# Later load landings, float32r products for the layer norm's sums, and split V loads in an attention, MLP and mixer kernel

## The chip, the cores and the metric

One core of a Trainium2 chip runs the whole computation as one program. The metric is the device time of one execution, in microseconds, as the median of several runs; a profiled execution gives the trace. TensorE (PE) does the matrix products, its weight loads (PEld) go beside them, VectorE (DVE), ScalarE (ACT) and GpSimd (POOL) do the element-wise work, and SyncE (SP) issues nearly all DMAs from one queue in order.

## The reference

Batch 4, 8 heads, 576 positions, head size 64, model width 512, hidden width 2048.

```python
scores = q @ k^T / sqrt(64);  bias = -(cum[i] - cum[j]) with cum = cumsum(max(s, 0))
attn = softmax(causal(scores + min(bias, 0)));  x = attn @ v          # heads side by side: x is (4, 576, 512)
xn = (x - mean(x)) / sqrt(var(x) + 1e-6) * g
x = x + relu(xn @ w1a) @ w2a                                           # first MLP, called layer 0
u = x + ((x^T @ U) @ V)^T                                              # mixer over the 576 positions, rank 32
out = u + relu(u @ w1b) @ w2b                                          # second MLP, called layer 1
```

## The kernel before

Work is cut into blocks of positions: for each batch b a block Ab of 256 positions and a block Bb of 320; in layer 1, blocks C0 to C3 of 512 positions and one block T0 that collects the last 64 positions of all four batches. Precision comes from splitting a float32 value into a float32r part (hi, a rounded copy) and the rest (lo, a subtraction); a product is then three float32r products, hi·hi, lo·hi and hi·lo. The helper `split` (line 384) issues the copy (`copy`, ACT line 381 or DVE line 382) and the subtraction (`tt`, DVE line 386 or POOL line 388).

The MLPs run as steps. One step is one block times one tile of 128 hidden units: `mlp1` (lines 1396 to 1398) forms the hidden tile in PSUM, ACT and DVE (lines 1402 and 1403) make its hi and lo parts, and `mlp2` (lines 1416 to 1418, or 1453 to 1455) adds its share of the output two steps later. Layer 0 has 128 steps in the order A0, A1 (steps 0 to 31, in turns of 8), A2, A3 (32 to 63), B0 (64 to 79), B1, B2, B3 (to 127). Layer 1 follows with C0, C1, C2, T0, C3. The attention and the layer norm of a later block run between the steps of earlier ones: the table `AT` gives the steps between which a block's attention is spread, and `LN` the step at which its layer norm is put. A0 and A1 have their attention ahead of the first step.

No engine's order is written by hand. `Plan` collects all operations with their data dependences, an assumed duration, a priority and the engines that may do each one. `plan` simulates them and keeps, for each engine, an order and a choice of engine; `latest` walks back from the end and gives each operation the latest start that delays nothing, and `issue` plans again (`PASSES` = 4 times) with those as priorities, less a head start `HEAD` in microseconds, found by the priority with which the operation was entered (-100 is A0's attention, -50 A0's layer norm, 1.5 A1's attention, 4.5 A1's layer norm, -4 and -3 weights). The shortest of the plans is emitted. The chip then runs each engine's list in that order, with semaphores for the dependences; the planned times themselves are not kept. In the plan, a DMA ends after a start-up, its bytes at 350 GB/s and the transfers ahead of it, and its reader is ready 1500 ns after that, plus an optional `lag`.

`layer_norm` (from line 969) serves blocks A2, A3 and B0 to B3. It needs two sums over the 512 features, which lie across partitions and four tiles: `ln_sum` adds the four tiles (three `tt`), and multiplies by a 128x128 matrix `ones` that holds 1/512, in plain float32 (line 967). The first sum gives the mean, the second the mean square. That is 12 sums in all. A0 and A1 use `layer_norm_tok`, which has no such product.

A `Pair` is two heads of one block. For a B block, its `load` (lines 636 to 663) brings q and k and, for each of two heads, V into a buffer `xs` of 128 rows and 320 columns, five key tiles of 64 columns. The fifth tile starts at key 448, so its first 64 rows repeat keys that the fourth tile has; the load brings all (line 661) and a POOL memset writes zeros over the repeated rows (line 663), after the load, since both write the same buffer. A split of V (`prep`, lines 382, 381, 386, 388) reads the buffer after that. `score` forms the scores (lines 747, 765, 769), DVE subtracts the mask and takes the extreme (lines 752, 773), ACT takes the exponential (783), the sums are inverted (790, 792), and `trans` transposes (823) into `pB`, for `pv` (867).

The lines around the sum and V's load are:

```python
pe(prio - 500, 4 * mm_cost(n), lambda: nc.tensor.matmul(ps[:, :n], ones.tile, into[:, :n], start=True, stop=True), [ones, into], [ps])
load(prio, 256 * nv, lambda a=a, v_in=v_in: nc.sync.dma_start(a[:, :w], v_in), [], [a], gate)
if blk == "B":
    P.op(prio, {"pool": (150, lambda a=a: nc.gpsimd.memset(a[:64, w - D:w], 0.0))}, [], [a])
```

Of the kernel before, what the change touches and what calls it, by code (L numbers as in the profile page):

```python
# [10 lines left out]
F32R = mybir.dt.float32r  # L11
I32 = mybir.dt.int32
U32 = mybir.dt.uint32
AF = mybir.ActivationFunctionType
ALU = mybir.AluOpType

B, H, S, D = 4, 8, 576, 64
# [14 lines left out]
LAST = ("C0", "C1", "C2", "T0", "C3")  # L32
W2SLOTS = 12

AT = {"A2": (1, 3), "A3": (1, 33), "B0": (26, 49), "B1": (50, 65), "B2": (67, 83), "B3": (83, 100)}
LN = {"A2": 9, "A3": 33, "B0": 62, "B1": 66, "B2": 84, "B3": 102}
W0 = (1, 14)
HEAD = {-100: -1, -50: 127, 1.5: 61, 4.5: 18, -4: 1, -3: -8}
W1 = (16, 60, 59)
PASSES = 4  # L40
AHEAD = 1500


def f(ap):
# [3 lines left out]
def mm_cost(n):  # L48
    return max(106.7, n / 2.4) + 13.3
# [39 lines left out]
class Plan:  # L89
# [196 lines left out]
    def issue(self, warm):  # L286
# [9 lines left out]
        for _ in range(PASSES):  # L296
            prio = self.latest(order, end)
            for o in self.ops:
                prio[o.seq] -= 1e3 * HEAD.get(o.prio, HEAD.get(o.prio + 500, 0))
            use = {e: [0.0] * NW for e in price}  # L300
# [35 lines left out]
def mha_ffn_mixer_ffn(ctx: ExitStack, tc, qkv_p, qkv_a, qkv_b, s, g, w1, w2, U, V, out):  # L336
    nc = tc.nc
    P = Plan(nc)
# [28 lines left out]
    def act(prio, n, fn, reads, writes, fixed=94):  # L367
        P.op(prio, {"act": (fixed + 0.8333 * n, fn)}, reads, writes)

    def pe(prio, cost, fn, reads, writes, hold=()):  # L370
        return P.op(prio, {"pe": (cost, fn)}, reads, writes, hold=hold)
# [2 lines left out]
        return 4 * max(n / 2.4, 53.3) + 2.5  # L374

    def load(prio, nbytes, fn, reads, writes, gate=None, rate=350.0, lag=0):
        P.op(prio, {"sp": (475, fn)}, reads, writes, nbytes, gate, rate=rate, lag=lag)

    def copy(prio, n, out, a, reads, writes, psum=False, soft=0.0, slow=False):
        P.op(prio, {  # L380
# [10 lines left out]
    def split(prio, n, hi, lo, src, reads, wh, wl, psum=False, soft=0.0, slow=False):  # L391
        copy(prio, n, hi, src, reads, wh, psum, soft, slow)
        tt(prio, n, lo, src, lambda: f(hi()), ALU.subtract, list(reads) + list(wh), wl, psum, soft)


    def fixed(name, shape, dtype=F32):
        return P.fixed(const.tile(shape, dtype, name=name))

    ident = fixed("ident", [128, 128])
    ones = fixed("ones", [128, 128])  # L400
    eps = fixed("eps", [128, 1])
    odd = fixed("odd", [128, 1])
    g_sb = fixed("g_sb", [128, KT])
    small = fixed("small", [128, 4])
# [14 lines left out]
    PRO = -1e6  # L419

    def setup():
        sc, cum = P.buf("xc", [128, 1280]), P.buf("v", [128, 1280])
        late = 5
        part = ((0, 256, PRO), (256, S, late))

        for c, (c0, c1, pr) in enumerate(part):
            for y in range(4):
                e, q = ("act", nc.scalar) if c == 0 and y % 2 else ("sp", nc.sync)
                P.op(pr, {e: (475, lambda y=y, c0=c0, c1=c1, q=q: q.dma_start(sc[R * y:R * (y + 1), c0:c1], s[:, c0:c1]))}, [], [(sc, ("s", c, y))], R * (c1 - c0) * 4)
        table = P.fixed(None)  # L430
        P.op(PRO, {"act": (1280, lambda: nc.scalar.preload_act_table_set("natural_log_exp_and_others"))}, [], [table])
        P.op(PRO, {"pool": (400, lambda: make_identity(nc, ident.tile))}, [], [ident])
        dve(PRO, 1, lambda: nc.vector.memset(eps.tile, 1e-6), [], [eps])
        dve(PRO, 1, lambda: nc.vector.memset(small.tile, 1e-9), [], [small])
        for a, z in ((0, 0.0), (R, 1.0), (2 * R, 0.0), (3 * R, 1.0)):
            dve(PRO, 1, lambda a=a, z=z: nc.vector.memset(odd[a:a + R], z), [], [(odd, "y%d" % a)])
        dve(PRO, 128, lambda: nc.vector.memset(ones.tile, 1.0 / DM), [], [ones], 0.521)
        P.op(PRO, {"pool": (600, lambda: nc.gpsimd.memset(causal.tile, 0.0))}, [], [causal])
        for y in range(4):
            act(PRO, R, lambda y=y: nc.scalar.activation(sel[R * y:R * (y + 1)], ident[R * y:R * (y + 1), R * y:R * (y + 1)], AF.Copy),  # L440
                [ident, table], [(sel, "y%d" % y)])

        def mask(d, n):
            return lambda: nc.gpsimd.affine_select(out=d, in_=d, compare_op=ALU.is_ge, fill=-8e9, base=0, pattern=[[-1, n]], channel_multiplier=1)

        P.op(PRO, {"pool": (266, mask(causal[:, 384:], 128))}, [causal], [causal])
        for c, (c0, c1, pr) in enumerate(part):
            k = [(sc, ("s", c, y)) for y in range(4)]
            dve(pr, c1 - c0, lambda c0=c0, c1=c1: nc.vector.tensor_scalar(out=sc[:, c0:c1], in0=sc[:, c0:c1], scalar1=0.0, scalar2=8.0, op0=ALU.max, op1=ALU.mult),
                k, k, 0.521)  # L450
            dve(pr, c1 - c0, lambda c0=c0, c1=c1: nc.vector.tensor_tensor_scan(
                cum[:, c0:c1], sc[:, c0:c1], sc[:, c0:c1], cum[:, c0 - 1:c0] if c0 else 0.0, ALU.add, ALU.max),
                k + [(cum, 0)] * c, [(cum, c)], 2.084)

        REL = {1: (sc, 576), 2: (sc, 832), 3: (sc, 0), 4: (cum, 640)}
        for i, (a, c) in REL.items():
            c0, c1 = COL[i], COL[i] + KEYS[i]
            pr = PRO if i == 1 else late
            key = [(a, ("s", c, y)) for c in range(2) for y in range(4)] if i == 3 else [(a, 10 + i)]

            def rel(y0=0, y1=4, a=a, c=c, i=i):
                return a[R * y0:R * y1, c:c + KEYS[i]]

            cums = [(cum, y) for y in range(1 + (i > 1))]
            end = lambda i=i: cum[:, KEYS[i] - 1:KEYS[i]]
            if i == 4:
                dve(pr, S, lambda end=end, rel=rel: nc.vector.tensor_scalar(out=rel(), in0=cum[:, :S], scalar1=end(), scalar2=None, op0=ALU.subtract), cums, key, 0.521, 128)
                load(pr, R * S * 4, lambda rel=rel: nc.sync.dma_start(cum_dr.tile, rel(0, 1)), key, [cum_dr])
                break
            dve(pr, KEYS[i], lambda i=i, end=end, rel=rel: nc.vector.tensor_scalar(  # L470
                out=rel().bitcast(F32R), in0=cum[:, :KEYS[i]], scalar1=end(), scalar2=odd.tile, op0=ALU.subtract, op1=ALU.mult),
                cums + [odd], key, 0.521, 128)
            dve(pr, KEYS[i], lambda i=i, c0=c0, c1=c1, end=end, rel=rel: nc.vector.scalar_tensor_tensor(
                out=ksum[:, c0:c1], in0=cum[:, :KEYS[i]], scalar=end(), in1=rel(), op0=ALU.subtract, op1=ALU.subtract),
                cums + key, [(ksum, i)], fixed=128)
        load(-1000, 2048, lambda: nc.sync.dma_start(g_sb.tile, g.rearrange("(k p) -> p k", p=128)), [], [g_sb])
        act(-1000, 4, lambda: nc.scalar.activation(g_sb.tile, g_sb.tile, AF.Copy, scale=-0.5), [g_sb], [g_sb])


    steps, runs = [], []  # L480
    for n, blocks in enumerate(GROUPS):
        for half in (n % 2, 1 - n % 2):
            for x in blocks:
                blk = (0, int(x[1]), x[0])
# [88 lines left out]
    def w2_ahead(m, gate):  # L573
        prio = NS0 + m - 8
        raw, t = w_raw(prio, 1, m, 1, gate, AHEAD), psum()
        f64_to_f32(prio, 512, lambda: t.tile, lambda: raw.tile, t, raw, psum=True)
# [40 lines left out]
    class Pair:  # L617
# [11 lines left out]
        def load(self, prio, gate):  # L629
            b, p, blk = self.b, self.p, self.blk  # L630
            nv = 128 * self.nj
# [26 lines left out]
            w = nv // 2  # L658
            for z, a in enumerate(self.vr):
                v_in = qkv_p[b, p, :, 512 + 128 * z:640 + 128 * z] if blk == "A" else qkv_b[b, 2 * p + z, :, 896:]  # L660
                load(prio, 256 * nv, lambda a=a, v_in=v_in: nc.sync.dma_start(a[:, :w], v_in), [], [a], gate)
                if blk == "B":
                    P.op(prio, {"pool": (150, lambda a=a: nc.gpsimd.memset(a[:64, w - D:w], 0.0))}, [], [a])

        def bounce(self, prio, gate):

# [294 lines left out]
    def ln_sum(prio, n, srcs, reads, into):  # L961

        for k in range(1, KT):
            tt(prio, n, lambda: into[:, :n], srcs[0] if k == 1 else lambda: into[:, :n], srcs[k], ALU.add,
               (reads[0] if k == 1 else [into]) + reads[k], [into])
        ps = psum()
        pe(prio - 500, 4 * mm_cost(n), lambda: nc.tensor.matmul(ps[:, :n], ones.tile, into[:, :n], start=True, stop=True), [ones, into], [ps])
        return ps

    def layer_norm(prio, b, blk):  # L970
# [551 lines left out]
    for st in range(NS0, NS, 2):  # L1522
        _, _, blk, m = steps[st]
# [25 lines left out]
    put(start1 - 12, lambda p, g: mix_prep_v(p, g))  # L1549
    for x in AT:  # L1550
        b, blk = int(x[1]), x[0]
        if x not in FULL:
            for p, pr in enumerate(pairs_of[b, blk]):
                put(max(0, AT[x][0] - 6 + p), lambda p, g, pr=pr: pr.bounce(p, g))
        spread(attn_items(b, blk), *AT[x])
        put(LN[x], lambda p, g, b=b, blk=blk: layer_norm(p, b, blk))
    for (l, b, blk), p in final.items():
        end = p + 1 + LAG
# [94 lines left out]
```

## Time and profile before

| | us |
|---|---|
| median of 3 runs | 1037.30 (1037.26 to 1037.39) |
| the profiled execution's own time | 1036.19 |
| its span, first to last instruction | 1034.4 |
| PE busy | 1017.1 (98%) |
| DVE busy | 694.6 (67%) |
| ACT busy | 470.2 (45%) |
| POOL busy | 138.5 (13%) |

The span leaves out 1.8 us around the program. A busy PE is one with a matmul in its pipeline; the distance from one matmul's start to the next tells its cost better than its duration, since they overlap. "Idle before" and "[0.81 <-DVE t L386]" name what ended a wait. SPq is the DMA queue of SyncE. Lines 381, 382, 386 and 388 are helpers, so the tile's name tells which operation is meant.

### The profile page before, as it was taken

To read this page: it belongs to the slowest core of one execution; us is meant where nothing else is said; L and a number is where in the kernel's file an instruction comes from. 1 tells how busy PE (TensorE), PEld (TensorE's weight loads), DVE (VectorE), ACT (ScalarE), POOL (GpSimd) and SP (SyncE) were. 2 spreads that over 40 slices of the span, in tenths; PEclk is the share of its full clock that TensorE was granted. 3 is DMA by queue.
4 is the path that set the end of the run, shared out by engine and by line. 5 is a ranking of instruction groups with operands and counts; after the bars stand their busy time and mean duration, and the time that the engine had idled before them with its cause. 6 is when DMAs were issued, how large, how long until landed. Compare 5 with 4: busy or idle time off the path is not lost.

```text
span 1034.4 us, 19312 instructions
## 1 busy us (share of the span) xinstructions
PE 1017.1 (98%) x7110; PEld 938.8 (91%) x7110; DVE 694.6 (67%) x1760; ACT 470.2 (45%) x1104; POOL 138.5 (13%) x288
## 2 busy tenths in 40 slices
PE   8999999999999999989999999999999999999998
PEld 7888888999999999979999999898999899899897
DVE  7999989866988878678754428547446645517444
ACT  6889877755856556557543314312111211112110
POOL 0021333511620222032100000001001000001000
PEclk9999999999999999999999999999999999999999
DMA  8999984668656976595475799981763576487851
GB/s 296 342 339 344 335 310 145 212 228 295 215 165 201 305 245 218 181 315 184 128 286 205 248 394 358 348 321 46 266 217 106 198 240 191 143 287 235 316 172 42
DMA packets 99231, 248.80 MB, mean 241 GB/s; under 512 B 16416, under 2 KB 47392, under 8 KB 94528
## 3 DMA queue, kind: packets, MB, share of 16 engines
q1 hardware_dynamic: 98464, 246.97, 69.6%
q8 instruction: 56, 0.92, 0.4%
q10 hardware_dynamic: 672, 0.59, 0.2%
q14 instruction: 39, 0.32, 0.1%
HBM read 193.97 MB, written 62.99 MB: 248 GB/s over the span
## 4 chain that ended last, share of the span: by engine, by line
PE 77%; DVE 5%; DMA 2%; ACT 2%; issue 1%; SPq 0%; DVEq 0%; POOL 0%; ACTq 0%; POOLq 0%
PE ps L1396 6%; PE ps L1398 5%; PE ps L1397 5%; PE ps L1309 5%; PE ps L1311 5%; PE ps L1310 5%; PE ps L867 4%; PE acc L1453 4%; PE acc L1454 4%; PE acc L1455 4%; PE ps L823 3%; PE acc L1347 3%; PE acc L1349 3%; PE acc L1348 3%; PE ps L1347 3%; PE ps L1348 3%
## 5 line engine op out<-in xcount | busy, mean ns | idle before, releaser
L1396 PE MATMUL ps<-xh,w 128*128 128x256 f32 (+1 forms) x512 | 157.8, 308 | 1.8 <-DVE pB L386 0.9
L1398 PE MATMUL ps<-xl,w 128*128 128x256 f32 (+1 forms) x512 | 151.3, 295 | 0.0
L1397 PE MATMUL ps<-xh,w 128*128 128x256 f32 (+1 forms) x512 | 151.2, 295 | 0.0
L1403 DVE SCALAR_TENSOR_TENSOR hl<-ps,hh 128x256 fp32r<-128x256 f32 (+1 forms) x144 | 64.5, 449 | 94.4 <-ACT hh L1402 94.0
L1402 ACT ACTIVATE hh<-ps 128x256 fp32r<-128x256 f32 (+1 forms) x144 | 58.2, 404 | 119.1 <-PE ps L1398 118.4
L1396 PEld LDWEIGHTS ps<-xh,w 128*128 128x128 f32 x512 | 96.7, 189 | 9.1 <-DVE pB L386 1.6
L1397 PEld LDWEIGHTS ps<-xh,w 128*128 128x128 f32 x512 | 96.8, 189 | 2.2
L1453 PE MATMUL acc<-hh,w 128*128 128x256 f32 (+1 forms) x320 | 97.3, 304 | 0.0
L1398 PEld LDWEIGHTS ps<-xl,w 128*128 128x128 f32 x512 | 96.6, 189 | 0.0
L1454 PE MATMUL acc<-hh,w 128*128 128x256 f32 (+1 forms) x320 | 93.8, 293 | 0.0
L1455 PE MATMUL acc<-hl,w 128*128 128x256 f32 (+1 forms) x320 | 93.8, 293 | 0.0
L1269 ACT ACTIVATE w<-hl 128x256 fp32r<-128x256 f32 x83 | 34.1, 418 | 124.7 <-DVE hl L1289 124.5
L783 ACT ACTIVATE t<-t,mx 128x384 f32<-128x384 f32 (+4 forms) x112 | 68.9, 617 | 47.0 <-DVE mx L773 39.2
L1289 DVE TENSOR_TENSOR hh<-ps,hh 128x256 f32<-128x256 f32 x64 | 27.1, 423 | 77.7 <-ACT hh L381 76.1
L1289 DVE TENSOR_TENSOR hl<-ps,hh 128x256 f32<-128x256 f32 x128 | 48.6, 419 | 44.9 <-PE ps L1311 43.7
L381 ACT ACTIVATE hh<-ps 128x256 f32<-128x256 f32 x31 | 12.0, 386 | 113.9 <-PE ps L1311 113.7
L386 DVE TENSOR_TENSOR pB<-ps,pB 128x384 fp32r<-128x384 f32 (+2 forms) x112 | 60.0, 569 | 5.2 <-ACT pB L381 4.7
L773 DVE CUSTOM_DVE_ANT_0 t<-ps,causal 128x128 f32<-128x128 f32 (+3 forms) x128 | 56.9, 484 | 8.5 <-PE ps L769 8.1
L1453 PEld LDWEIGHTS acc<-hh,w 128*128 128x128 f32 x320 | 60.7, 190 | 1.5 <-issue 1.0
L1454 PEld LDWEIGHTS acc<-hh,w 128*128 128x128 f32 x320 | 60.7, 190 | 0.5
L1455 PEld LDWEIGHTS acc<-hl,w 128*128 128x128 f32 x320 | 60.6, 190 | 0.0
L1295 DVE SCALAR_TENSOR_TENSOR w<-hl,w 128x256 fp32r<-128x256 f32 x128 | 52.3, 426 | 6.6 <-ACT w L1269 5.7
(258 smaller groups left out, 2894.8 us busy)
## 6 DMA issues: line engine op xcount, KB each, us to landing
w<-w_dr SPq DMA_DIRECT2D x112, 512.0 KB, 7.3
pB<-w_dr SPq DMA_DIRECT2D x36, 1024.0 KB, 5.4
qk<-w_dr SPq DMA_DIRECT2D x28, 768.0 KB, 5.2
w_dr<-w SPq DMA_DIRECT2D x32, 512.0 KB, 6.0
w_dr<-wr SPq DMA_DIRECT2D x32, 512.0 KB, 4.8
wr<-w1a SPq DMA_DIRECT2D x16, 512.0 KB, 6.3
wr<-w2a SPq DMA_DIRECT2D x16, 512.0 KB, 6.2
wr<-w1b SPq DMA_DIRECT2D x16, 512.0 KB, 6.5
```

Source lines behind the costliest of these rows:

```text
L386: alts = {"dve": (68 + 1.042 * n, lambda: nc.vector.tensor_tensor(out=out(), in0=a(), in1=b(), op=op))}
L783: act(prio, K, lambda t=t, mx=mx, o=o, K=K, x=x, y=nt * z + x: nc.scalar.activation(t[:, o:o + K], t[:, o:o + K], AF.Exp, bias=mx[:, (1 if ...
L1289: dve(st - 1000, 256, lambda: nc.vector.tensor_tensor(out=d.tile, in0=region(r), in1=a.tile, op=ALU.add), [p, a], [d])
L1347: nc.tensor.matmul(aa[z].tile, w[:, 0, sl], h[:, 0], start=first, stop=False)
L1348: nc.tensor.matmul(aa[z].tile, w[:, 1, sl], h[:, 0], start=False, stop=False)
L1396: nc.tensor.matmul(ps[:, :n], lhs(k, 0), xh[:, k, :n], start=k == 0, stop=False)
L1397: nc.tensor.matmul(ps[:, :n], lhs(k, 1), xh[:, k, :n], start=False, stop=False)
L1398: nc.tensor.matmul(ps[:, :n], lhs(k, 0), xl[:, k, :n], start=False, stop=k == KT - 1)
L1403: dve(st - 1000, n, lambda: nc.vector.scalar_tensor_tensor(out=hl[:, :n], in0=ps[:, :n], scalar=0.0, in1=f(hh[:, :n]), op0=ALU.max, op1=AL ...
L1453: nc.tensor.matmul(a, w[:, 0, sl], hh[:, :n], start=new, stop=False)
L1454: nc.tensor.matmul(a, w[:, 1, sl], hh[:, :n], start=False, stop=False)
L1455: nc.tensor.matmul(a, w[:, 0, sl], hl[:, :n], start=False, stop=last and (z == 1 or blk == "B"))
```

## The change

Five edits. Every load and store entered with a positive priority is planned as landing at least 1000 ns later than before. The layer norm's sum is split into hi and lo parts, and two float32r products with a rounded copy `mean_w` of the matrix replace the one float32 product. `AT` and `LN` move a few blocks' attention and layer norm by a step or two. `HEAD` gives A0's layer norm, A1's attention and A1's layer norm smaller head starts. For B blocks, the zeros are written ahead of the load and apart from it, and the load comes as two: four whole key tiles, and the lower 64 rows of the fifth.

```diff
-AT = {"A2": (1, 3), "A3": (1, 33), "B0": (26, 49), "B1": (50, 65), "B2": (67, 83), "B3": (83, 100)}
-LN = {"A2": 9, "A3": 33, "B0": 62, "B1": 66, "B2": 84, "B3": 102}
+AT = {"A2": (1, 3), "A3": (1, 32), "B0": (26, 49), "B1": (50, 65), "B2": (67, 84), "B3": (85, 100)}
+LN = {"A2": 9, "A3": 32, "B0": 62, "B1": 66, "B2": 85, "B3": 102}
-HEAD = {-100: -1, -50: 127, 1.5: 61, 4.5: 18, -4: 1, -3: -8}
+HEAD = {-100: -1, -50: 117, 1.5: 41, 4.5: 16, -4: 1, -3: -8}
+LATE = 1000
     def load(prio, nbytes, fn, reads, writes, gate=None, rate=350.0, lag=0):
-        P.op(prio, {"sp": (475, fn)}, reads, writes, nbytes, gate, rate=rate, lag=lag)
+        P.op(prio, {"sp": (475, fn)}, reads, writes, nbytes, gate, rate=rate, lag=max(lag, LATE if prio > 0 else 0))
+    mean_w = fixed("mean_w", [128, 128], F32R)
+        act(PRO + 1, 128, lambda: nc.scalar.activation(mean_w.tile, ones.tile, AF.Copy), [ones], [mean_w])
-                load(prio, 256 * nv, lambda a=a, v_in=v_in: nc.sync.dma_start(a[:, :w], v_in), [], [a], gate)
-                if blk == "B":
-                    P.op(prio, {"pool": (150, lambda a=a: nc.gpsimd.memset(a[:64, w - D:w], 0.0))}, [], [a])
+                if blk == "A":
+                    load(prio, 256 * nv, lambda a=a, v_in=v_in: nc.sync.dma_start(a[:, :w], v_in), [], [a], gate)
+                    continue
+                P.op(prio, {"pool": (150, lambda a=a: nc.gpsimd.memset(a[:64, w - D:w], 0.0))}, [], [(a, "zero")])
+                load(prio, 256 * (nv - 128), lambda a=a, v_in=v_in: nc.sync.dma_start(a[:, :w - D], v_in[:, :w - D]), [], [(a, "most")], gate)
+                load(prio, 128 * 128, lambda a=a, v_in=v_in: nc.sync.dma_start(a[64:, w - D:w], v_in[64:, w - D:]), [], [(a, "end")], gate)
-        pe(prio - 500, 4 * mm_cost(n), lambda: nc.tensor.matmul(ps[:, :n], ones.tile, into[:, :n], start=True, stop=True), [ones, into], [ps])
+        parts = [P.buf("ls", [128, 320], F32R) for _ in range(2)]
+        def mm():
+            for z, a in enumerate(parts):
+                nc.tensor.matmul(ps[:, :n], mean_w.tile, a[:, :n], start=z == 0, stop=z == 1)
+        split(prio, n, lambda: parts[0][:, :n], lambda: parts[1][:, :n], lambda: into[:, :n], [into], [parts[0]], [parts[1]])
+        pe(prio - 500, 2 * mm_cost(n), mm, [mean_w] + parts, [ps])
```

## Rows read from the trace of the kernel before

**Rows 1.** The page: busy time, share of the span and instructions of each engine.

```profile
PE 1017.1 (98%) x7110; PEld 938.8 (91%) x7110; DVE 694.6 (67%) x1760; ACT 470.2 (45%) x1104; POOL 138.5 (13%) x288
```

**Rows 2.** Waits of PE: engine, line, releaser: total us, times, longest.

```profile
PE ps L747 <- DVE mx L773: 2.0, 1, 2.0
...
PE ps L1396 <- DMA pB<-w_dr: 1.3, 1, 1.3
...
PE ps L1244 <- DVE t L386: 0.8, 1, 0.8
```

**Rows 3.** Windows: stretch, length, then busy PE, PEld, DVE, ACT, POOL, clock, DMA.

```profile
6.00:37.00 31.00, 28.26 (x247) 23.40 (x246) 28.19 (x115) 25.29 (x62) 0.41 (x2) 1.00 0.97 350
37.00:66.00 29.00, 28.96 (x216) 26.06 (x216) 28.66 (x78) 26.90 (x64) 4.66 (x7) 1.00 0.96 340
...
207.00:316.00 109.00, 109.00 (x889) 104.79 (x888) 85.54 (x219) 68.61 (x161) 31.25 (x72) 1.00 0.64 217
```

**Rows 4.** The sum's product (line 967): source view: times, then min, median and max ns.

```profile
L967 PE MATMUL ps<-ls,ones x24: 377/431/475, 119.1 to 538.2; 128*128 128x320 f32 x16, 128*128 128x256 f32 x8
```

**Rows 5.** Timeline of PE, B3's second sum: start us, us, operation.

```profile
537.93 0.70 PE L967 MATMUL ps<-ls,ones 128*128 128x320 f32 x2
538.23 0.55 PE L1396 MATMUL ps<-xh,w 128*128 128x320 f32 x1
538.62 0.31 PE L1397 MATMUL ps<-xh,w 128*128 128x320 f32 x1
538.77 0.31 PE L1398 MATMUL ps<-xl,w 128*128 128x320 f32 x1
```

**Rows 6.** Timeline, 436 to 448 us: parts of a split of 320 columns, DVE and POOL.

```profile
441.60 0.49 DVE L386 TENSOR_TENSOR xc<-xc,ls 128x320 f32<-128x320 f32 x1
...
442.01 0.32 DVE L382 CAST xh<-xc 128x320 fp32r<-128x320 f32 x1
...
444.55 0.88 POOL L388 TENSOR_TENSOR xl<-xc,xh 128x320 fp32r<-128x320 f32 x1
```

**Rows 7.** Timeline, 187 to 208 us: A3's last low part, its first step.

```profile
194.00 0.41 DVE L386 TENSOR_TENSOR xl<-xc,xh 128x256 fp32r<-128x256 f32 x1
...
206.65 0.28 PE L1396 MATMUL ps<-xh,w 128*128 128x256 f32 x1
```

**Rows 8.** Timeline, 437 to 448 us: V's load, its zeros, its split, the stall.

```profile
437.59 0.33 SPq L661 DMA_DIRECT2D xs<-qkv_b  x1
...
444.29 0.14 POOL L663 MEMSET xs<- 64x64 f32 x1 [2.60 <-DMA xs<-qkv_b]
...
444.47 0.49 DVE L382 CAST v<-xs 128x320 fp32r<-128x320 f32 x1 [2.15 <-POOL xs L663]
...
446.76 0.68 DVE L773 CUSTOM_DVE_ANT_0 t<-ps,causal 128x512 f32<-128x512 f32 x1
...
447.50 1.28 PE L747 MATMUL ps<-qk 128*128 128x288 f32 x6 [1.98 <-DVE mx L773]
```

**Rows 9.** Waits of POOL for V's load: total us, times, longest.

```profile
POOL xs L663 <- DMA xs<-qkv_b: 69.6, 17, 20.4
```

**Rows 10.** DMA issues: count, KB each, median us to landing.

```profile
xs<-qkv_b SPq DMA_DIRECT2D x32, 160.0 KB, 4.0
...
qk<-qkvB SPq DMA_DIRECT2D x16, 16.0 KB, 4.3
```

**Rows 11.** Timeline of PE ahead of the first step, and that step.

```profile
30.74 1.09 PE L1010 MATMUL ps<-ident,xs 128*128 128x128 f32 x8 [0.80 <-DVE mx L773]
...
36.97 0.38 PE L1396 MATMUL ps<-xh,w 128*128 128x256 f32 x1
```

**Rows 12.** Groups of DVE by line, 6 to 37 us: busy us, mean ns, idle.

```profile
L773 DVE CUSTOM_DVE_ANT_0 t<-ps,causal 128x128 f32<-128x128 f32 (+1 forms) x30 | 8.8, 344 | 2.8 <-PE ps L769 2.8
...
L382 DVE COPY pB<-ps 128x384 f32<-128x384 f32 x4 | 2.2, 541 | 0.0
L913 DVE TENSOR_TENSOR x<-ps,rc 128x256 f32<-128x256 f32 x5 | 2.1, 415 | 0.0
```

## The prediction

> **What bounds the kernel now.** I read the page's busy times first: PE is busy for 98% of the span, DVE for 67% [rows 1]. So time is won only where PE's own work shrinks or where it stands still. Next the waits of PE. They are few: the longest is 2.0 us, and 1.3 and 0.8 us stand at operations that need a load [rows 2]. Then the windows, to see who stands close behind PE. From 37 to 66 us PE is busy 28.96 of 29 us and DVE 28.66, so there DVE has no room; from 207 to 316 us PE is busy throughout and DVE 85.5 of 109, so there element-wise work is free within reason. Ahead of the first MLP step, from 6 to 37 us, DVE is busy 28.2 and ACT 25.3 of 31 us, and DMA is at 0.97. The granted clock is 1.00 in each of these stretches [rows 3]. The base of the sum is the profiled execution, 1036.2 us (span 1034.4, and 1.8 around it); that is 1.1 us under the median of 1037.3, and I carry the differences over to the median.
>
> **The layer norm's sums.** There are 12; the trace shows 24 products, two for each sum, 8 sums of 320 columns and 4 of 256 [rows 4]. What one costs PE is read from the starts around it: from 537.93 to 538.62 us lie the sum and one float32r product, and such a product is 0.15 us from the next (538.62 to 538.77). So the sum costs 0.69 - 0.15 = 0.54 us [rows 5]. Two float32r products of the same width cost 0.30 by the same step. The gain is 0.24 us for each wide sum, and by width 0.19 for a narrow one: 8 x 0.24 + 4 x 0.19 = 2.7 us. Since PE has next to no idle time where most of them lie, this goes straight off the end. A2's two sums lie where DVE also is near its limit; if nothing is won on any narrow sum it is 1.9 us, my lower end.
>
> Each sum gains a split of its own: a copy, 0.32 us on DVE, and a subtraction of 0.49 on DVE or 0.88 on POOL [rows 6]. All on DVE that is 12 x 0.81 = 9.7 us, spread over 120 to 540 us, where DVE has such gaps as the 23.5 us of 207 to 316 [rows 3]. The chain to the normalised block grows twice by a split and its hand-overs, 2 x (0.81 to 1.20) less the shorter products, 1.1 to 1.9 us; half as much again for hand-overs, an estimate, makes it under 3 us. The work that hides it is the preceding block's steps. The tightest block is A3, whose last low part starts at 194.0 and whose first step at 206.65, 12 us later [rows 7]. I cost it at nothing; if the cover were gone it would be up to 3 us for one block. The rounded copy of the matrix is one ACT operation of 128 columns, under the longest of rows 6, and first needed at 119.1 us [rows 4].
>
> **Later landings, and V.** The plan lets a reader of V's 160 KB run 3.07 us after the issue begins (1.10 of start-up, 0.47 for the bytes at 350 GB/s, 1.50 to the reader); the median landing is 4.0 [rows 10]. Adding 1.0 makes the plan agree with the median. What the mistake costs is seen at 445 us. V's load is issued at 437.59 and the zeros start at 444.29, after 2.6 us of waiting; the cast of V has kept DVE waiting 2.15 us by then. The scores' reduction (line 773) is queued behind that cast on DVE, starts only at 446.76, and PE stands still for 1.98 us for the PSUM that it frees [rows 8]. Here the load took 6.7 us, so 1.0 us alone doesn't cover it; but the order is remade, and the reduction need only be placed ahead of the cast. I expect the stall to go more likely than not, between 0 and 2.0 us, and take 1.5. The zeros themselves are 0.14 us plus a hand-over; that the cast waits for the load remains.
>
> Ahead of the load, the zeros no longer hold POOL, which waits 69.6 us in 17 places for V [rows 9]. Behind them on POOL stand masks, sums and subtractions that DVE and ACT need. POOL is 13% busy, so I give this 0 to 1 us, and take 0.2. Against it stand 32 more DMA issues on SP's queue, 0.33 us each [rows 8], 10.6 us over some 360; what is queued behind one, mostly weights and the next q and k, goes out 0.33 us later for each. V is whole when its smaller part is: 16 KB transfers with the same short rows land in 4.3 us against 4.0 for the 160 KB ones [rows 10]. With the later issue V comes 0.3 + 0.3 = 0.6 us later, inside the added 1.0. The cover is that allowance; without it, 0.6 us falls on as many stalls like that of 445 us as there are, one now. I bound it by 0 and 0.6, and take 0.1 lost.
>
> The Trainium skill speaks against this edit: DMA: Bandwidth & Descriptors, Specifications, has transfers under 512 B fall below line rate, and V's second part consists of 256-byte rows. The 16 KB transfers of rows 10 have such rows too and need 0.3 us more than one ten times their size, so the trace agrees in direction. If all 32 second parts delayed PE by that much, the sum would lose 9.6 us, which would need PE to wait for each of them.
>
> Of the other waits that follow a load, the 0.8 us at line 1244 has a load of the mixer's rows ahead of its split: 0 to 0.8, I take 0.4. The 1.3 us for `pB<-w_dr` is a load whose buffer comes free late, so it can't be issued earlier by being planned later: 0 to 1.3, I take 0.2. Both waits are in [rows 2]. So far 1.5 + 0.2 - 0.1 + 0.4 + 0.2 = 2.2 us won. But every engine's list is planned anew, and a new order makes its own stalls. The nearest price for one is the 0.8 to 2.0 us of rows 2. I take 0.6 lost, with ends 2.5 lost and 0.7 won.
>
> **The intervals and head starts.** B3's attention gets 15 steps in place of 17, A3's 31 in place of 32; both lie where PE is full and DVE has gaps, so nothing. The smaller head start for A1's attention lets it drift past the first step. In the old order PE waits 0.80 us for A0's normalised rows with A1's reductions among the work ahead, and the first step starts at 36.97 [rows 11]. One A1 pair is worth four reductions, a copy and a normalisation on DVE, 4 x 0.344 + 0.541 + 0.415 = 2.3 us [rows 12]. Moved out whole, it would start the first step up to 2.3 us earlier, but 37 to 66 us has 0.34 us of DVE to spare [rows 3], so the same work is met again before A1's steps. I bound this by 2.3 won and 2.3 lost, and take 0.5 won.
>
> **The sum.** 2.7 + 2.2 - 0.6 + 0.5 = 4.8 us. 1036.2 - 4.8 = 1031.4 for a profiled execution; as the median 1037.3 - 4.8 = 1032.5 us. Its own range, from 1.9 on the sums with 1 from the rest up to 2.7 with 6 from the rest, is 1028.6 to 1034.4.
>
> **Rivals.** (a) Only the products pay: the stalls trade places, the start stays, and 1.0 to 2.7 us remains: 1034.6 to 1036.3, around 1035.2. For it speaks that PE's waits are few and small, so one or two new ones undo what is won; against it, that the largest wait hangs on just the landing that is now planned later. (b) Slower: A1's attention, started later, isn't done when its steps come, and DVE, full from 37 us on, can't catch up. The place is step 8, at about 66 us. It decides as soon as the work moved past the first step exceeds what the start gave back plus 0.34 us. Two pairs moved with nothing given back are 2 x 2.3 = 4.6 us; with the products' 2.7 and 0.6 of new stalls that is 1037.3 + 4.6 - 2.7 + 0.6 = 1039.8. For it speaks DVE's 28.66 of 29; against it, that DVE's total work before step 8 stays the same. (c) The start gives its whole 2.3 us and both DMA waits and the 445 us stall go: 2.7 + 2.3 + 2.0 + 0.8 + 1.3 = 9.1, about 1028.2. (d) The change doesn't do what it says: the weight load before each product, no longer hidden, makes the float32r pair as dear as the old one. PE then wins nothing on the sums: 1037.3 - 2.1 = 1035.2. Against it: products of this kind, each with its own weights, already follow each other by 0.15 us [rows 5].
>
> **Chances.** Forecast 0.46, (a) 0.24, (b) 0.18, (c) 0.10, (d) 0.02. About 0.2%, 2.1 us, is what a measurement of this kernel can tell from no change, so the bounds are 1035.2 and 1039.4. Faster takes the forecast, (c) and somewhat under half of (a) and (d), 0.66; the rest of these and a quarter of (b) are the same, 0.19; slower 0.15. For 8 in 10 the range reaches from 1028.5, into (c), to 1038.0, over (a) and a part of (b).
>
> **What the profile will show.** Two float32r products for each sum, 0.30 us from first start to the next product, and PE busy some 3 us shorter. No POOL wait for V's load. No wait of about 2 us at line 747 behind a cast of V; if it stands elsewhere with the same chain, the step on landings was wrong. The first step's start, against 36.97, tells the head starts; if it is earlier and PE's waits between 37 and 130 us have grown by as much, the work only moved. The forecast fails if PE's waits after the start sum to more than now, by 3 us or more.

## The result: 10.7 us faster, more than twice what was forecast

The changed kernel takes 1026.6 us in the median (1026.3 to 1027.6, 4 runs) against 1037.35 of the kernel before beside it. The ratio is 0.9897, with a 95% interval of 0.9880 to 0.9914. The forecast was 1032.5 with 1028.5 to 1038.0 around it. The sign was right, and the time lies 1.9 us under the lower end.

The page of the changed kernel, busy time by engine (to be read against [rows 1]):

```profile
PE 1014.7 (99%) x7116; PEld 938.0 (92%) x7116; DVE 682.5 (67%) x1734; ACT 481.4 (47%) x1132; POOL 164.0 (16%) x311
```

PE does 2.4 us less. That alone can't be 9.9 us of span (1034.4 to 1024.5), so most of the gain is in the time in which PE stood still. The windows tell how much. The stretch is from the start of the first MLP product to the start of the last product; the columns are its bounds, its length and the busy time of PE, PEld, DVE, ACT and POOL. First the kernel before, then the changed one:

```profile
36.97:1030.10 993.13, 983.91 (x6844) 912.36 (x6844) 662.93 (x1632) 442.75 (x1038) 136.34 (x276) 1.00 0.70 238
```

```profile
34.23:1020.21 985.98, 982.79 (x6856) 912.68 (x6856) 652.86 (x1614) 454.45 (x1065) 161.91 (x299) 1.00 0.69 240
```

So the span is made up of three parts: the first product comes 2.74 us earlier (36.97 to 34.23), PE is idle afterwards for 3.19 us in place of 9.22, which is 6.03 less, and PE's busy time in the stretch falls by only 1.12 us, since 12 more products lie in it (6856 for 6844). Together 9.9 us.

The waits of PE in the changed kernel (line, releaser: total us, times, longest), to be read against [rows 2]:

```profile
PE acc L1617 <- DVE ones L439: 1.5, 1, 1.5
PE ps L1410 <- ACT wr L382: 1.0, 1, 1.0
PE ps L771 <- DVE w L387: 0.5, 1, 0.5
PE ps L1410 <- DVE pB L383: 0.5, 1, 0.5
```

The 1.5 us is the start of the program. The 2.0 us at the scores, the 1.3 us for `pB<-w_dr` and the 0.8 us at the mixer are gone. So is a wait of the kernel before that [rows 2] doesn't show, between layer 0 and layer 1, which I had left out as unrelated to a load:

```profile
PE ps L1309 <- DVE x L1463: 1.3, 1, 1.3
```

The longest wait after the first step is now the 1.0 us ahead of T0, and that one is new.

The second sum of B3, on the timeline of PE (start, us, operation), to be read against [rows 5]:

```profile
525.28 0.46 PE L978 MATMUL ps<-ls,mean_w 128*128 128x320 f32 x2
525.57 0.31 PE L1410 MATMUL ps<-xh,w 128*128 128x320 f32 x1
525.72 0.30 PE L1411 MATMUL ps<-xh,w 128*128 128x320 f32 x1
```

From the first of the two products to the next operation are 0.29 us; 0.30 was forecast. V's two loads stand in the list of DMA issues with 3.5 and 3.9 us to landing (count, KB each, median us), where [rows 10] had 4.0 for the whole:

```profile
xs<-qkv_b SPq DMA_DIRECT2D x32, 128.0 KB, 3.5
xs<-qkv_b SPq DMA_DIRECT2D x32, 16.0 KB, 3.9
```

### The profile page after: what moved, and what is told of

The parts are those of the page before. It is cut to its first block, busy times and chain, and to the rows that moved or that the text cites. A ratio compares the mean times of both kernels' runs of the same rounds, so it can differ in the third digit from the quotient of the medians.

```text
span 1024.5 us, 19498 instructions
## 1 busy us (share of the span) xinstructions
PE 1014.7 (99%) x7116; PEld 938.0 (92%) x7116; DVE 682.5 (67%) x1734; ACT 481.4 (47%) x1132; POOL 164.0 (16%) x311
## 3 DMA queue, kind: packets, MB, share of 16 engines
q1 hardware_dynamic: 101024, 246.45, 69.6%
## 4 chain that ended last, share of the span: by engine, by line
PE 87%; DVE 6%; DMA 5%; ACT 1%; issue 1%; SPq 0%; POOL 0%; DVEq 0%; ACTq 0%; POOLq 0%
PE ps L1410 7%; PE ps L1412 6%; PE ps L1411 6%; PE ps L1323 5%; PE ps L1325 5%; PE ps L1324 5%; PE ps L873 5%; PE ps L829 4%; PE acc L1467 4%; PE acc L1468 3%; PE acc L1469 3%; PE acc L1361 3%; PE acc L1363 3%; PE acc L1362 3%; PE ps L1361 3%; PE ps L1362 3%
## 5 line engine op out<-in xcount | busy, mean ns | idle before, releaser
L779 DVE CUSTOM_DVE_ANT_0 t<-ps,causal 128x256 f32<-128x256 f32 (+3 forms) x128 | 56.7, 485 | 9.0 <-PE ps L775 8.1
```

## The experiments

Every edit gives the planner other durations, priorities or operations, so all engines' lists are made anew, except in changed_again and float32_in_place. Three theories were set against each other. Theory 1, landings: the old order was planned on landings that come later on the chip, and planning them later removes the waits. Theory 2: each edit pays its own small amount. Theory 3, redraw: any new order differs by some microseconds, whatever the edit is for.

On the chips of the experiments, single runs of one kernel spread over more microseconds than above, so the comparison is the ratio to the kernel before on the same chip. The last three columns come from one profiled execution of each, by the same windows as above.

| run | ratio, 95% interval | first step at, us | PE busy from there, us | PE idle from there, us |
|---|---|---|---|---|
| before | 1 | 36.97 | 983.9 | 9.2 |
| changed | 0.9897, 0.9880 to 0.9914 | 34.23 | 982.8 | 3.2 |
| changed_again | 0.9892, 0.9869 to 0.9915 | 33.49 | 983.0 | 3.7 |
| late_alone | 0.9966, 0.9950 to 0.9982 | 33.51 | 988.4 | 5.8 |
| sums_alone | 0.9949, 0.9929 to 0.9969 | 36.71 | 982.8 | 6.7 |
| all_but_late | 0.9951, 0.9931 to 0.9971 | 37.03 | 982.3 | 8.0 |
| all_but_sums | 0.9966, 0.9946 to 0.9986 | 33.21 | 986.0 | 6.7 |
| all_but_v | 0.9879, 0.9859 to 0.9899 | 33.78 | 983.3 | 3.6 |
| all_but_intervals | 0.9925, 0.9904 to 0.9946 | 33.88 | 984.5 | 7.3 |
| all_but_head | 0.9910, 0.9876 to 0.9945 | 33.20 | 984.0 | 3.3 |
| three_edits | 0.9904, 0.9883 to 0.9925 | 34.32 | 981.2 | 2.9 |
| float32_in_place | 0.9912, 0.9888 to 0.9935 | 36.49 | 985.5 | 3.4 |
| late_500 | 0.9931, 0.9913 to 0.9949 | 37.29 | 983.2 | 4.9 |
| late_900 | 0.9920, 0.9896 to 0.9944 | 34.65 | 982.7 | 7.1 |
| late_1100 | 1.0000, 0.9981 to 1.0019 | 33.50 | 991.1 | 6.8 |
| late_2000 | 1.0048, 1.0029 to 1.0067 | 33.06 | 992.8 | 10.9 |
| lag1400_no_late | 1.0043, 1.0026 to 1.0060 | 36.18 | 984.3 | 15.5 |
| lag1600_no_late | 0.9975, 0.9955 to 0.9994 | 36.19 | 980.5 | 8.9 |
| lag1400_late | 0.9929, 0.9913 to 0.9945 | 34.18 | 982.0 | 7.2 |
| lag1600_late | 0.9973, 0.9958 to 0.9989 | 35.18 | 983.4 | 9.4 |

### Later landings, alone and left out

In late_alone, the kernel before has only the edit below; in all_but_late the changed kernel has everything else.

```diff
+LATE = 1000        # all_but_late: LATE = 0
-        P.op(prio, {"sp": (475, fn)}, reads, writes, nbytes, gate, rate=rate, lag=lag)
+        P.op(prio, {"sp": (475, fn)}, reads, writes, nbytes, gate, rate=rate, lag=max(lag, LATE if prio > 0 else 0))
```

> The kernel before with one edit: loads and stores are planned 1000 ns later. Theory 1 (landings): the order of before stalls because it was planned on landings that come later on the chip, so this edit alone wins most of the 10.7 us that the sums do not explain: 1028 to 1031 us, with no wait of 2 us at the scores behind a cast of V. Theory 2 (each part pays a little): 1034 to 1036. Theory 3 (redraw: any new order differs by some us, whatever the edit is for): anywhere from 1030 to 1040, with new waits unrelated to loads.

> The changed kernel with the added 1000 ns taken back; the sums, V, intervals and head starts stay. Theory 1 (landings): loses most of the gain that is not the sums', 1031 to 1035 us, and PE's waits after the start sum to 6 us or more again. Theory 2 (each part pays): loses 1 to 3 us, 1027.5 to 1029.5. Theory 3 (redraw): 1024 to 1036, no rule.

Alone the edit wins 0.34%, 3.5 us of 1037, and left out it costs 0.5%. All_but_late is at 1032.5, inside theory 1's figure, and idle for 8.0 us again; theory 3's wider range holds it too. But late_alone, with 1033.3, is slower than theory 1 had it, though its first step comes 3.5 us earlier: 42 more products lie behind the first step (x6886 for x6844), and PE is busy there for 988.4 us in place of 983.9. There the earlier start is work moved. Theory 2's figures, 1027.5 to 1029.5 and 1034 to 1036, hold neither median. In both runs the first step tells whether the allowance is there: 33.5 with the edit, 37.0 without. The count of products behind it is firmer than its time: 6844 or 6845 in all five orders without the allowance, 6855 or more in every order with one.

The wait of 2 us at the scores is gone in late_alone, as theory 1 had it. That doesn't speak for theory 1, because it is gone in sums_alone and all_but_late as well, which have no later landings; no other order of these experiments has it.

### The sums, alone, left out, and in place

Sums_alone has only the edit of `ln_sum` and its matrix; all_but_sums has all the others. In float32_in_place the planner sees the changed kernel with its durations and data dependences, so that no list is ordered anew; only the products differ. It leaves the lo parts out of the sums.

```diff
-            for z, a in enumerate(parts):
-                nc.tensor.matmul(ps[:, :n], mean_w.tile, a[:, :n], start=z == 0, stop=z == 1)
+            nc.tensor.matmul(ps[:, :n], ones.tile, f(parts[0][:, :n]), start=True, stop=True)
```

> The kernel before with one edit: the layer norm's sums by two float32r products of hi and lo parts. All theories give the products 2.7 us by the starts in the trace: 1034.6 us. Theory 3 (redraw) lets the time scatter by 3 us or more around that, 1031 to 1038, as waits of PE change places.

> The changed kernel with the layer norm's sums in plain float32 again. Theories 1 and 2: 2.7 us slower than the changed kernel, 1029.3 us. Theory 3 (redraw): 1027 to 1034, with the difference in PE's waits and not in the products.

> The changed kernel with every list in the same order, the splits still made, and each sum as one float32 product of the hi part in place of the two float32r products; the lo parts are left out of the sums. It measures the products alone, without a new order. By the starts in the trace 8 x 0.24 + 4 x 0.19 = 2.7 us slower than the changed kernel, 1029.3 us. If the products are hidden by waits of PE it is 1 us or less; if the sums owe their gain mostly to the new order, all_but_sums loses far more than this one.

The in-place run is the clean one. Its window, to be read against the changed kernel's above:

```profile
36.49:1025.37 988.88, 985.45 (x6857) 913.80 (x6856) 652.67 (x1614) 454.91 (x1065) 161.63 (x299) 1.00 0.69 239
```

PE is idle for 3.4 us, as in the changed kernel, and busy for 985.45 in place of 982.79: the products' price is 2.66 us (2.4 against changed_again's 983.02), where 2.7 was worked out. The ratio is 0.15% above the changed kernel's, 1.6 us, but the intervals overlap, so the time alone doesn't settle it. The two other runs move by more than that: sums_alone wins 0.51%, 5.3 us, and all_but_sums lacks 0.69% of the changed kernel's gain, 7.2 us. What is beyond 2.7 stands in PE's idle time, 6.7 us in each against 9.2 before and 3.2 in the changed kernel. That is not the products; it is the order.

One thing in this run warns against single profiles. Its lists have the changed kernel's order, and yet its first step comes at 36.49 in place of 34.23. A wait for the first weights' split has grown to 1.80 us:

```profile
24.92 0.32 PE L771 MATMUL ps<-ksum,sel 64*128 64x128 f32 x1 [1.80 <-DVE w L387]
```

In the changed kernel the same wait took 0.5 us, so 1.3 of the 2.3 us stand here. The start can thus move by 2 to 3 us between executions of one order (changed_again, at 33.49, and this run were on different chips).

### V, the intervals and the head starts, left out

Each is the changed kernel with one edit undone; three_edits undoes V's and the head starts' together.

```diff
 # all_but_v, three_edits: V's load whole again, its zeros after it
 # all_but_intervals
-AT = {"A2": (1, 3), "A3": (1, 32), "B0": (26, 49), "B1": (50, 65), "B2": (67, 84), "B3": (85, 100)}
-LN = {"A2": 9, "A3": 32, "B0": 62, "B1": 66, "B2": 85, "B3": 102}
+AT = {"A2": (1, 3), "A3": (1, 33), "B0": (26, 49), "B1": (50, 65), "B2": (67, 83), "B3": (83, 100)}
+LN = {"A2": 9, "A3": 33, "B0": 62, "B1": 66, "B2": 84, "B3": 102}
 # all_but_head, three_edits
-HEAD = {-100: -1, -50: 117, 1.5: 41, 4.5: 16, -4: 1, -3: -8}
+HEAD = {-100: -1, -50: 127, 1.5: 61, 4.5: 18, -4: 1, -3: -8}
```

> The changed kernel itself, beside those that leave out one edit: 1026 to 1029 us, ratio to the kernel before 0.988 to 0.992.

> The changed kernel with V loaded whole and its zeros written after the load, as before. Theory 1 (landings): with landings planned later, V's load is rarely late, so V's edit adds little: 0 to 1.5 us slower than the changed kernel, and POOL waits for V's load in the trace again for 20 us or more. Theory 3 (redraw: any new order differs by some us): 2 to 5 us slower, with new waits of PE that V has no part in.

> The changed kernel with the old intervals for the attention of A3, B2 and B3 and their layer norms. Theory 1 (landings): the intervals hide under steps either way, 0 to 1 us slower than the changed kernel. Theory 3 (redraw; the intervals were picked together with the rest): 2 to 5 us slower.

> The changed kernel with the old head starts, 127, 61 and 18. My prediction gave them 0.5 us, between 2 won and 2 lost, by an earlier first step. If the first step comes where it comes in the changed kernel, that step is wrong and what remains is redraw: 0 to 4 us slower.

> The kernel before with later landings, the sums and the intervals; V's load and the head starts as before. If V and the head starts give nothing, by mechanism, and the order happens to stay a good one: ratio to the kernel before 0.988 to 0.991, idle of PE after the first step under 5 us. Theory 3 (redraw): ratio 0.988 to 1.000, since this order is drawn anew too.

V's edit gives nothing that can be told: 0.9879 without it, 0.9892 with it, the intervals lying over each other. And yet POOL's wait for V's load is back in all_but_v (total us, times, longest), as in [rows 9]; in the changed kernel that row doesn't exist:

```profile
POOL xs L666 <- DMA xs<-qkv_b: 52.9, 17, 19.1
```

So 53 us of POOL standing still cost PE nothing that can be told. The head starts give nothing that can be told either (0.9910), and above all they don't bring the first step: it comes at 33.20 with the old ones. They hardly change the order: PE's list in all_but_head differs from the changed kernel's in 43 of 7116 places, in all_but_v in 2632. Three edits without these two are as good as all five (0.9904).

The intervals cost 0.33% when left out, 3.4 us, though the two ratios' 95% intervals overlap; theory 3 had 2 to 5 us, theory 1 at most 1. PE is idle for 7.3 us in place of changed_again's 3.7, and the trace shows where half of that stands: in B2's attention PE waits 1.77 us for the scores' place in PSUM. The timeline of that stretch, DVE and then PE:

```profile
368.66 0.36 DVE L383 CAST qk<-qk 128x384 fp32r<-128x384 f32 x1 [1.97 <-DMA qk<-qkvB]
368.94 1.89 DVE L387 TENSOR_TENSOR qk<-qk 128x576 fp32r<-128x576 f32 x2
...
370.85 0.49 DVE L886 TENSOR_TENSOR x<-ps,x 64x320 f32<-64x320 f32 x1
```

```profile
371.40 0.67 PE L753 MATMUL ps<-qk 128*128 128x288 f32 x3 [1.77 <-DVE x L886]
```

This is the chain of [rows 8] with other names. DVE is held for 1.97 us by a load that lands late (here q and k, there V), then does the splits, and behind them is queued the operation that frees PSUM for PE. The load's parts land 7.3 to 8.1 us after their issues. In the changed kernel they take no less, 7.8 to 8.6 us; there DVE frees PSUM ahead of any split of q and k, and PE doesn't wait:

```profile
368.33 0.49 DVE L886 TENSOR_TENSOR x<-ps,x 64x320 f32<-64x320 f32 x1
```

```profile
369.82 0.56 PE L753 MATMUL ps<-qk 128*128 128x288 f32 x3
```

So it is the order that decides here, and the landing is as late in both.

### The allowance by size, and the order drawn again

```diff
-LATE = 1000
+LATE = 500         # late_900, late_1100, late_2000 likewise
```

> The changed kernel with landings planned 500 ns later in place of 1000. Theory 1 (landings): between the changed kernel and the one without (1032.5), about 1029 to 1030, PE's idle time after the first step 5 to 6 us. Theory 3 (redraw): 1024 to 1034, no order by size.

> The changed kernel with landings planned 900 ns later in place of 1000. Theory 1 (landings): no reason for a difference over 1 us, 1026 to 1028. Theory 3 (redraw: a new order differs by some us, whatever the edit is for): 1024 to 1034, with other waits of PE. It measures what a new order is worth by itself.

> The changed kernel with landings planned 1100 ns later in place of 1000. Theory 1 (landings): within 1 us of the changed kernel, ratio 0.988 to 0.992. Theory 3 (redraw): ratio 0.988 to 1.002, idle of PE after the first step 3 to 12 us; with late_900, lag1400_late and lag1600_late it gives the spread of equal allowances.

> The changed kernel with landings planned 2000 ns later in place of 1000. Theory 1 (landings): the landing is hardly ever later than planned, so PE waits no more for loads than in the changed kernel, but its work is spread more loosely: 1025 to 1029. Theory 3 (redraw): 1024 to 1036. If the allowance only moves work past the first step, the first step comes earlier still and the time is not lower.

From no allowance over 500 and 900 to 1000 ns the ratio falls as theory 1 has it, 0.9951, 0.9931, 0.9920 and 0.9897, though neighbours can't be told apart; at 1100 and 2000 it jumps to 1.0000 and 1.0048. Late_900 and late_1100 differ from the changed kernel by a tenth of the allowance, and theory 1 wanted them within 1 us; they lose 0.28% and 1.08% to changed_again, 2.9 and 11.2 us, and the second is clear of the intervals. Late_2000 is slower than the kernel before, and slower than either theory had it. In late_1100 and late_2000 some 8 to 10 us of it are work moved past the first step: PE is busy there for 991.1 and 992.8 us. Ahead of the first step stand 86 idle-time products in both, whose results nothing uses; the changed kernel has 60. By line, late_1100 and then the changed kernel (busy us, mean ns):

```profile
L1617 PE MATMUL acc<-ones 128*128 128x256 bf16 x86 | 12.2, 304 | 1.5 <-DVE ones L439 1.5
```

```profile
L1617 PE MATMUL acc<-ones 128*128 128x256 bf16 x60 | 9.4, 323 | 1.5 <-DVE ones L439 1.5
```

A first step at 33.5 is thus no gain by itself: attention was put off, and PE ran on idle-time products in its place. The longest wait of late_1100 has the form seen twice by now, with an allowance larger than that of the changed kernel:

```profile
471.42 0.36 DVE L383 CAST qk<-qk 128x384 fp32r<-128x384 f32 x1 [2.40 <-DMA qk<-qkvB]
...
473.09 0.48 DVE L1417 SCALAR_TENSOR_TENSOR hl<-ps,hh 128x320 fp32r<-128x320 f32 x1
```

```profile
473.62 2.13 PE L873 MATMUL ps<-pB,v 128*128 128x320 f32 x7 [2.74 <-DVE hl L1417]
```

The last four runs draw the order anew by 100 ns in another planned lag, in the changed kernel and in the one without the allowance. It belongs to the raw weights of layer 1 and two loads of the mixer. The allowance is the larger of a load's own lag and 1000 ns, not an addition, so these loads, with 1500, are not planned later by it. The bias rows have half of that lag, 750 ns: the allowance moves them by 250 only, and in the two runs without it they change by 50.

```diff
-AHEAD = 1500
+AHEAD = 1400       # lag1600_...: 1600
```

> The changed kernel without the added 1000 ns, its order drawn anew by planning 1400 in place of 1500 ns for some loads of layer 1. Theory 1 (landings): like all_but_late, ratio to the kernel before 0.993 to 0.997, PE idle for 6.5 us or more after the first step, first step at about 37 us. Theory 3 (redraw): ratio 0.988 to 1.000, idle 3 to 10 us.

> As lag1400_no_late, with 1600 ns. Theory 1 (landings): ratio 0.993 to 0.997, idle 6.5 us or more after the first step. Theory 3 (redraw): ratio 0.988 to 1.000, idle 3 to 10 us.

> The changed kernel, its order drawn anew by planning 1400 in place of 1500 ns for some loads of layer 1. Theory 1 (landings): near the changed kernel, ratio to the kernel before 0.988 to 0.992, PE idle for 3 to 5 us after the first step. Theory 3 (redraw): ratio 0.988 to 1.000, idle 3 to 10 us, as the group without the 1000 ns.

> As lag1400_late, with 1600 ns. Theory 1 (landings): ratio 0.988 to 0.992, idle 3 to 5 us after the first step. Theory 3 (redraw): ratio 0.988 to 1.000, idle 3 to 10 us.

A change of 100 ns moves the ratio from 0.9951 to 1.0043 and 0.9975 without the allowance, and from 0.9892 to 0.9929 and 0.9973 with it. All four lie outside theory 1's ranges; three lie in theory 3's, and lag1400_no_late is worse than either had it. The draw is worth up to 0.9%, 9.5 us: nearly as much as the whole change. In lag1600_late the longest wait is again a late load, the rows of the bias, which hold DVE ahead of the reduction that PE waits for:

```profile
373.26 0.46 DVE L758 CUSTOM_DVE_ANT_0 t<-ps,t 128x288 f32<-128x288 f32 x1 [2.94 <-DMA t<-cum_dr]
```

```profile
373.78 0.55 PE L829 MATMUL ps<-ident,t 128*128 128x128 f32 x3 [1.98 <-DVE mx L758]
```

Over all the traces nine waits of PE after the first step are 1.5 us or longer. Six have this form: DVE held by a load, with PE's release queued behind (the four shown, late_alone's 1.9 and late_2000's 1.5 us). The loads of the four landed 6.6 to 9.4 us after their issues, far more than the 1000 ns cover. Two of the nine, of 1.6 us, wait for a load directly, and one has neither form. They are 1.5 to 2.7 us each, of 5 to 15 us of idle time in those orders.

By size, the five orders without the allowance leave PE idle after the first step for 6.7 to 15.5 us, 9.7 in the mean (9.2, 6.7, 8.0, 15.5, 8.9); the eleven different ones with 900 to 1100 ns for 2.9 to 9.4, 5.8 in the mean. So the allowance seems worth about 4 us of idle time, but the groups overlap. In the four pairs that differ by the 1000 ns alone it wins 0.34, 0.54, 1.14 and 0.02%.

The waits by their place divide the 6.0 us. This table has PE's waits (us) between the layers for `x` (line 1309 of the kernel before), at the mixer (1244), for `pB<-w_dr` and at T0's first products, from the lists of waits and the timelines:

| run | between the layers | mixer | `pB<-w_dr` | start of T0 |
|---|---|---|---|---|
| before | 1.3 | 0.8 | 1.3 | 0 |
| sums_alone | 0.8 | 0.6 | 1.2 | 0 |
| all_but_late | 1.0 | 0 | 0.6 | 0 |
| lag1400_no_late | 0.6 | 0.5 | 1.6 | 0 |
| lag1600_no_late | 1.0 | 1.0 | 1.4 | 0 |
| changed | 0 | 0 | 0 | 1.2 |
| the 14 others with an allowance | 0, but 0.4 in lag1600_late | 0 to 0.1 | 0, but 0.7 in all_but_v, 0.6 in all_but_intervals | 0.8 to 1.6 |

The first three waits together are 1.6 to 3.4 us in every order without the allowance and 0 to 0.7 in every order with one; the fourth comes with it. So 3.4 us less 1.2, 2.2 us of the 6.0, follow the allowance. The load of `pB<-w_dr` itself is no faster: the second one after T0's start takes 7.6 us from issue to landing before (906.38 to 913.99) and 7.8 us in the changed kernel (896.75 to 904.52), but there PE has other products until 904.56. How the allowance makes the other two waits go was not followed.

The other 3.8 us, among them the 2.0 at the scores that no other order has, follow no edit. Outside these four places PE is idle for 5.8 us in the kernel before, for 2.0 in the changed kernel and about as little in all_but_head, all_but_v and three_edits, and for 4.1 to 12.8 us in the thirteen other orders, with an allowance and without. So V's edit and the head starts have no part in it. The sums, the new intervals and the 1000 ns don't secure it either: lag1400_late and lag1600_late have all five edits, and are idle for 7.2 and 9.4 us in all. That the changed kernel has so little is the luck of its draw, as far as these runs show. With 2.7 us at the products and 1.2 to 1.3 from the earlier start (below), this is the whole 9.9 us of span.

## Why the prediction was too small

**The sums: right.** 2.7 us was worked out, and 2.4 to 2.7 measured with the order kept. The added splits hide, as costed: the list of waits of the changed kernel has none of 0.5 us or more that the longer chain would explain.

**Landings and the new order: the size wrong, and the cause for the most part.** I took 2.2 us won at single waits and 0.6 lost to new stalls, 1.6 in all, with 6 won as the outer end of everything but the products. PE's idle time after the first step fell by 6.0. The step that failed is the pricing of the new order, 0.6 lost with ends 2.5 lost and 0.7 won. I listed the waits that a load had caused directly and left the others standing, as the 1.3 us between the layers, and let the new order add stalls of its own. But an order drawn anew loses the old one's waits and gets its own number of them: here 3.2 us, in other draws up to 15.5. The three waits that I had listed went whole, 4.1 us where I took 2.1; the rest, which I had at 0.6 lost, measured 1.9 won. A range for the two together should have run from some 6 lost to 6 won, with the idle time of the old order, 9.2 us, as its natural upper end.

The mechanism was right only in part. The chain at 445 us was read rightly, and the same chain stands in five other orders. But my 1.5 us for it were credited to the later landing, and it went in every other order, with the allowance or without. What the runs show for the landing is 2.2 us at other places, where I had 0.4 for the mixer, 0.2 for `pB<-w_dr` and nothing for the wait between the layers. The remaining 3.8 us are a good draw, which nothing in the prediction could have told.

**V: worth nothing that can be told.** I gave POOL's release 0.2 us and the second issue 0.1 lost. The run without the edit can't be told from the run with it. The 445 us stall stays away in all_but_v too, where V's zeros come after the load again, so its going is not V's edit. The Trainium skill, in DMA: Bandwidth & Descriptors, Specifications, has transfers under 512 B fall below line rate. The trace agrees with that in direction only: the small part needs 3.9 us against 3.5 for the part eight times its size.

**Intervals and head starts: wrong in the cause.** I gave 0.5 us to the head starts by an earlier first step. The first step did come 2.7 us earlier, but all_but_head has it too and all_but_late doesn't. It is the allowance that moves work behind the first step: A1's loads have a positive priority and get it, A0's don't. What moved is not a whole pair of A1, as I had it, but 12 products (line 902, the last products of a pair; of the 96 of A0 and A1, 72 lay ahead of the first step before, not all as the section on the kernel before has it, and now 60), 0.11 us each by the distance of their starts, some 1.4 us. So the earlier start gave 1.3 us net. That figure is of one execution: changed_again starts at 33.49, and the same order at 36.49 in float32_in_place. The intervals, costed at nothing, cost 3.4 us when undone, half of it by a late load that another order met.

**The rivals.** (c), the full gain at the start and all load waits gone, at 1028.2, came nearest; I gave it 0.10. Its three waits did go whole, but the start gave less than its 2.3 us, and the draw made up for that. (b), A1's attention moved out and met again, isn't what happened here. Late_1100 and late_2000 show a part of it, at 991.1 and 992.8 us of PE's time and ratios of 1.0000 and 1.0048: the work is met again as PE's own, not as a wait at step 8 (late_1100's PE is idle for 0.3 us from 33.5 to 130). My reason against it, that the total stays the same, overlooked that the time ahead of the first step is then filled with products whose results nothing uses.

## What to carry to other kernels

Where a program plans its order from assumed times, price an edit in two parts: what it saves with the order kept, which the trace of before gave here to a few tenths of a microsecond, and a new draw of the order, whose spread here was as large as the idle time that the old order had on the bounding engine. Before one credits an edit with more than its own part, draw the order again by a number that shouldn't matter, and undo the edits one by one. Then compare the waits place by place: one that stands in every order without the edit and in hardly any with it is the edit's, and one that goes in every new order isn't. Look for an in-order engine that waits for a load while something that the bounding engine needs is queued behind it; planning loads 1000 ns later did not rule it out here.

## What was not expected of the hardware

One order gives different starts: from the same lists, the first MLP product came at 34.23, 33.49 and 36.49 us (the last with float32 sums, which lie later, and on another chip than the second); 1.3 us of the difference stand at the split of the first weights, and the rest was not followed. And 52.9 us of waiting on POOL [rows 9 had 69.6] cost the bounding engine nothing that could be measured.
